# The order of the last group's stores, and of the last tile's second half on TensorE, in a fused attention and MLP kernel

## The chip, the cores and the metric

The kernel runs on one core of one Trainium2 chip. The metric is device time in microseconds (us) of one execution. The median of the three timed runs of the kernel before is 219.3 us (219.28 to 220.8). The profile is of one execution on its own, and has its own time.

## The reference

Two stages are computed one after the other. The first is a linear attention with a decay: for 4 batches and 8 heads of 768 positions and 64 columns, block by block, with a state that is carried from block to block. The second is an MLP on the 3072 rows that come out of it, with 512 columns in and out and 2048 in between:

```python
for b in range(nb):                     # 12 blocks of 64 positions
    intra = np.einsum('bhic,bhjc->bhij', qb, kb) * Dmask[None]
    intra = np.einsum('bhij,bhjd->bhid', intra, vb)
    inter = np.einsum('bhid,bhde->bhie', qb * lam_pow[None], kv_state)
    out[:, :, sl] = intra + inter
    kv_state = lam_block * kv_state + np.einsum('bhsd,bhse->bhde', kb_dec, vb)

h = x @ w_in                            # (3072, 512) @ (512, 2048)
s = np.sin(alpha * h)
g = h + s * s / (alpha + 1e-09)
return (g @ w_out).astype(np.float32)   # (3072, 2048) @ (2048, 512)
```

Only the last product and its way to memory are touched by the change.

## The kernel before, in words

The 3072 rows are worked in six groups of 512, numbered 0 to 5. For each group the attention part leaves its result transposed in a tile `xt`. The first MLP product (`f1`) makes 16 blocks of 128 of the 2048 middle columns, each with four matmuls (L689). ScalarE takes the sine (L696), ScalarE or GpSimd the square (L703, L705), and VectorE combines both into the tile `gall` (L708). The second product (`f2`) makes the output of the group in four row tiles, m = 0 to 3, each of 128 rows and 512 columns.

One row tile of `f2` is 16 matmuls that add up in one PSUM bank, in four blocks of four (`f2_g_m_j`, L725). A block takes as its weights four 128x128 pieces of `gall`, and multiplies them with 512 columns of `w_out_sb`. When the fourth block is done, ScalarE copies the bank to a buffer `ob` in SBUF (`ev_g_m`, L731). SyncE (SP) then issues two stores of 64 rows each, 128 KB each (`out_g_m`, L753).

The last row tile, group 5 and m = 3, is made differently (`make_f2_end`). It is cut into two halves of 256 columns, a and b, and each half has a bank of its own and four blocks of four matmuls (`f2_5_3_0a` to `f2_5_3_3a`, and the same with b). Half a is copied by ScalarE (`end0`, L737), and SP issues its two stores of 64 KB (`send0`, L746). Half b is copied by VectorE (`end1`, L739). Of its two stores (`send1`, L746) SP issues the first and ScalarE's queue the second:

```python
add("send0", on("SP", 1.0), [ev], lambda op, ev=ev, cols=cols:
    f2send(op, ev, g, m, cols, (SY, SY)))
...
add("send1", on("SP", 1.0), [ev], lambda op, ev=ev, cols=cols:
    f2send(op, ev, g, m, cols, (SY, A)))
```

What runs in what order is written out by hand. `SEQ` (L173 to L277) holds one list of names for each engine, SP among them. `Plan.run` walks the five lists with estimated costs, gives each operation its buffers, and emits the instructions in the order of the starts that it works out. Each engine therefore runs its own list in order. A waiting instruction holds everything behind it on the same engine. The waits themselves follow from the data: a copy waits for the matmuls of its bank, a store for its copy, and a copy for the stores that last read its `ob` buffer. There are three `ob` buffers (`NOB = 3`, L286), and the plan never gets back the one that `end0` takes.

The end of the five lists before the change is this:

- TensorE (L204, L205): three blocks of tile 1, the b half's first two blocks between the first and the second block of tile 0, and the b half's last two blocks at the very end. Tile 2 and the a half stand ahead of these.
- ScalarE (L253, L254): the copies `ev_5_2 end0 ev_5_1 ev_5_0`.
- VectorE (L223): `end1`.
- SP (L276): the stores `out_5_2 out_5_1 send1 send0 out_5_0`.

Of the kernel before, what the change touches and what calls it, by code (L numbers as in the profile page):

```python
# [145 lines left out]
def kernel(  # L146
# [59 lines left out]
        "DVE":  # L206
# [70 lines left out]
    }  # L277
    QS = set()
    CK0 = [("ACT", .62), ("DVE", .43)]
# [792 lines left out]
```

## Time and profile before

| what | value |
|---|---|
| timed runs, median of three | 219.3 us (219.28 to 220.8) |
| the profiled execution's own time | 218.37 us |
| its span, from the first to the last instruction | 216.6 us |
| TensorE (PE) busy | 206.4 us, 95% of the span |
| ScalarE (ACT) busy | 139.1 us, 64% |
| GpSimd (POOL) busy | 131.4 us, 61% |
| VectorE (DVE) busy | 119.4 us, 55% |
| stores of 128 KB that SP issues (L753) | 46, median 2.4 us from issue to landing |
| stores of 64 KB that SP issues (L746) | 3, median 2.0 us |
| stores of 64 KB that ScalarE's queue issues (L746) | 1, 2.2 us |

The span is what the trace covers, and 1.77 us of the execution's own time lie around it. Times of single instructions are given in us from the start of the span. The engines' busy times leave out the issuing of DMAs, the waits and the barrier at the end. So a stretch in which all engines are idle can still be work: stores that are issued, in flight, or waited for. "PEq", "SPq" and the like are the sequencers of the engines, which issue and wait.

### The profile page before, as it was taken

Reading aid. Unit: us, or ns where it says so; the run is one execution under the profiler, and the core shown is the slowest. Engines: PE = TensorE matmul, PEld = TensorE weight load, DVE = VectorE, ACT = ScalarE, POOL = GpSimd, SP = SyncE. Lnnn points to the kernel's source line nnn. Section 1 sums busy time; section 2 is a strip of 40 time slices with the busy share of each in tenths; the row PEclk is TensorE's granted clock in tenths of the full one; section 3 lists DMA queues with packets and bytes.
Section 4 is the critical chain, followed back from the end, with each engine's and each line's share of the span. In section 5 each row is a group of like instructions: output and inputs, shape, how many; then the busy total and the mean of one; then the engine's idle time right before and its main releaser. Section 6 shows DMA issues by size and latency. Waiting matters only on the chain.

```text
span 216.6 us, 5232 instructions
## 1 busy us (share of the span) xinstructions
PE 206.4 (95%) x2066; PEld 105.6 (49%) x2066; DVE 119.4 (55%) x174; ACT 139.1 (64%) x251; POOL 131.4 (61%) x212
## 2 busy tenths in 40 slices
PE   8889999999999999999999999999999999999970
PEld 3466444555445555455545555544444444445430
DVE  3487775385488754777958868773555223022000
ACT  3675788554998668979887787567587635442210
POOL 7999899488799789998979998231511120011000
PEclk9999999999999999999999999999999999999996
DMA  6999999999998999999888740042040120044424
GB/s 176 300 278 207 206 157 200 304 251 305 246 278 221 182 273 250 249 190 293 224 201 203 128 100 3 0 100 48 0 97 2 25 61 14 0 97 92 99 55 98
DMA packets 62139, 33.65 MB, mean 155 GB/s; under 512 B 17938, under 2 KB 59170, under 8 KB 62114
## 3 DMA queue, kind: packets, MB, share of 16 engines
q1 hardware_dynamic: 57776, 29.04, 57.9%
q0 software_dynamic: 4224, 4.19, 12.3%
q8 instruction: 16, 0.26, 0.5%
q10 hardware_dynamic: 114, 0.07, 0.1%
q14 instruction: 9, 0.07, 0.1%
HBM read 27.27 MB, written 6.29 MB: 155 GB/s over the span
## 4 chain that ended last, share of the span: by engine, by line
PE 87%; POOL 5%; DVE 2%; issue 2%; ACT 1%; POOLq 0%; DVEq 0%
PE hps L689 38%; PE ops L725 35%; PE okv L725 3%; PE sp L532 3%; PE okv L655 3%; PE okv L642 2%; POOL vb L498 1%; DVE gall L708 1%; PE okv L566 1%; PE pt L508 1%; POOL E L410 1%; ACT s L696 1%; ACT s L703 1%; DVE sm L540 1%; POOL w_in_sb L456 0%
## 5 line engine op out<-in xcount | busy, mean ns | idle before, releaser
L708 DVE SCALAR_TENSOR_TENSOR gall<-s,r_sb,hps 128x512 bf16<-128x512 bf16 (+1 forms) x97 | 69.6, 740 | 60.1 <-ACT s L703 42.9
L689 PE MATMUL hps<-xt,w_in_sb 128*128 128x512 bf16 (+1 forms) x388 | 91.7, 377 | 0.7 <-DVE gall L708 0.6
L696 ACT ACTIVATE s<-hps,alpha_sb 128x512 bf16<-128x512 f32 (+1 forms) x97 | 65.5, 680 | 29.0 <-PE hps L689 27.5
L725 PE MATMUL ops<-w_out_sb,gall 128*128 128x512 bf16 (+1 forms) x368 | 83.1, 370 | 0.0
L705 POOL TENSOR_TENSOR s<-s 128x512 bf16<-128x512 bf16 x31 | 32.1, 1041 | 49.3 <-ACT s L696 47.2
L725 PEld LDWEIGHTS <-gall 128*128 128x128 bf16 x400 | 38.5, 98 | 42.1 <-DVE gall L708 0.2
L689 PEld LDWEIGHTS <-w_in_sb 128*128 128x128 bf16 x388 | 36.4, 98 | 42.1 <-issue 1.8
L703 ACT ACTIVATE s<-s 128x512 bf16<-128x512 bf16 (+1 forms) x66 | 40.3, 621 | 1.2
L540 DVE TENSOR_TENSOR sm<-sp,mask 128x1024 bf16<-128x1024 f32 x24 | 29.2, 1218 | 1.0 <-PE sp L532 1.0
L498 POOL TENSOR_TENSOR vb<-st_v,R 128x512 bf16<-128x512 f32 x24 | 25.0, 1045 | 1.1 <-DMA st_v<-in_v_dram 0.9
L731 ACT COPY ob<-ops 128x512 f32<-128x512 f32 x21 | 12.2, 586 | 19.7 <-PE ops L725 19.7
L594 POOL TENSOR_TENSOR kvbd<-kvx,LBD 128x256 bf16<-128x256 f32 x32 | 19.7, 614 | 2.5
L674 DVE TENSOR_TENSOR xt<-okv,ET 128x512 bf16<-128x512 f32 x24 | 16.5, 687 | 6.1 <-ACT kva L576 3.6
L591 POOL TENSOR_TENSOR kvx<-kva,kvs 128x128 f32<-128x128 f32 x32 | 14.6, 456 | 7.3 <-ACT kva L576 7.2
L492 POOL CAST qk<-st_k 128x512 bf16<-128x512 f32 x18 | 10.9, 614 | 3.3 <-DMA st_k<-in_k_dram 3.2
L532 PE MATMUL sp<-qt 64*64 64x128 bf16 x384 | 10.1, 221 | 0.1
L655 PE MATMUL okv<-sm,vb 64*64 64x128 bf16 x384 | 9.7, 218 | 0.5 <-DVE sm L540 0.5
L490 ACT CAST qk<-st_q 128x512 bf16<-128x512 f32 x13 | 7.9, 619 | 3.1 <-DMA st_q<-in_q_dram 3.1
L576 ACT COPY kva<-okv 128x256 f32<-128x256 f32 (+1 forms) x16 | 5.1, 316 | 6.9 <-PE okv L566 6.9
L632 POOL TENSOR_TENSOR kvs<-kvx,ET 128x128 f32<-128x128 f32 x24 | 9.4, 404 | 0.0
L762 PE MATMUL bz<-const-bfloat16-1.0 128*128 128x256 bf16 (+1 forms) x33 | 8.3, 358 | 0.8 <-PEq L1056 0.8
L642 PEld LDWEIGHTS <-kvbd 128*128 128x128 bf16 x80 | 6.2, 98 | 5.3 <-POOL kvbd L594 0.5
(63 smaller groups left out, 109.5 us busy)
## 6 DMA issues: line engine op xcount, KB each, us to landing
st_k<-in_k_dram SPq DMA_DIRECT2D x24, 256.0 KB, 4.0
st_q<-in_q_dram SPq DMA_DIRECT2D x24, 256.0 KB, 5.1
st_v<-in_v_dram SPq DMA_DIRECT2D x24, 256.0 KB, 4.4
out_dram<-ob SPq DMA_DIRECT2D x46, 128.0 KB, 2.4
w_out_sb<-in_moe_w_out_dram POOLq DMA_DIRECT2D x4, 512.0 KB, 8.5
w_in_sb<-in_moe_w_in_dram POOLq DMA_DIRECT2D x2, 512.0 KB, 7.2
w_in_sb<-in_moe_w_in_dram POOLq DMA_DIRECT2D x1, 768.0 KB, 10.2
w_in_sb<-in_moe_w_in_dram POOLq DMA_DIRECT2D x1, 256.0 KB, 7.1
```

The source lines that it names most:

```text
L498: ENGINE[op.eng].tensor_tensor(out=T[u, "vb"][:], in0=T[u, "v"][:].rearrange("p h two e -> p two h e"), in1=R[:, :, hs].unsqueeze(3).to_br ...
L532: nc.tensor.matmul(out=T[u, "sp"][half[c], hd, par, hp, :], lhsT=QT[half[hd], 1, par, hp, half[c]], rhs=QT[half[hd], 0, :, hp, half[c]], s ...
L540: V.tensor_tensor(out=T[u, "sm"][:].rearrange("p hd par hp i -> p (hd par) hp i"), in0=T[u, "sp"][:].rearrange("p hd par hp i -> p (hd par ...
L594: G.tensor_tensor(out=bd[:], in0=X.unsqueeze(2).to_broadcast([P, 2, 2, D]), in1=LBD[:, hs, :].unsqueeze(3).to_broadcast([P, 2, 2, D]), op= ...
L655: nc.tensor.matmul(out=okv[half[hd], c, hp * P:(hp + 1) * P], lhsT=VB[half[c], par, 2 * hp + hd, :], rhs=ST[half[c], hd, par, hp, :], star ...
L674: V.tensor_tensor(out=o, in0=i, in1=ET[:, 2 * hh:2 * hh + 2].rearrange("p hp two e -> p hp (two e)") .unsqueeze(1).to_broadcast([P, 2, 2, ...
L689: op.ins = nc.tensor.matmul(out=op.tile[:, cols], lhsT=w_in_sb[:, c, f * P:(f + 1) * P], rhs=xt[g][:, c].rearrange("p b c i -> p (b c i)") ...
L696: A.activation(out=op.tile[:, cols], in_=mm.tile[:, cols], func=ACTF.Sin, scale=alpha_sb[:, f:f + 1])
L703: A.activation(out=op.tile[:, cols], in_=s1, func=ACTF.Square)
L705: ENGINE[op.eng].tensor_tensor(out=op.tile[:, cols], in0=s1, in1=s1, op=ALU.mult)
L708: V.scalar_tensor_tensor(out=gall[g][:, f, cols], in0=sq.tile[:, cols], scalar=r_sb[:, f:f + 1], in1=mm.tile[:, cols], op0=ALU.mult, op1=A ...
L725: op.ins = nc.tensor.matmul(out=first.tile[:, cols], lhsT=gall[g][:, f, m * P:(m + 1) * P], rhs=w_out_sb[:, f, cols], start=(f == 0), stop ...
```

## The change

In `SEQ`, two lists are written in another order. No instruction is added or taken away in the source, and no size changes.

- TensorE: the last three blocks of tile 0 move ahead of the b half's first two blocks, so that the b half is one block of 16 matmuls behind all full tiles.
- SP: `send0` moves ahead of `out_5_1`, and `send1` moves behind `out_5_0`. The list ends `out_5_2 send0 out_5_1 out_5_0 send1`.

In the built program ScalarE's and VectorE's instructions keep their order; SP's list and TensorE's differ as the diff says.

```diff
@@ -202,7 +202,7 @@
             "f2_5_3_0a f2_5_3_1a f2_5_2_1 f2_5_3_2a f2_5_3_3a f2_5_1_1 f2_5_2_2 f2_5_2_3 f2_5_1_2 "
-            "f2_5_0_0 f2_5_1_3 f2_5_3_0b f2_5_3_1b f2_5_0_1 f2_5_0_2 f2_5_0_3 f2_5_3_2b f2_5_3_3b ",
+            "f2_5_0_0 f2_5_1_3 f2_5_0_1 f2_5_0_2 f2_5_0_3 f2_5_3_0b f2_5_3_1b f2_5_3_2b f2_5_3_3b ",
@@ -273,7 +273,7 @@
-            "out_3_3 out_2_0 out_2_3 out_4_3 out_5_2 out_5_1 send1 send0 out_5_0 ",
+            "out_3_3 out_2_0 out_2_3 out_4_3 out_5_2 send0 out_5_1 out_5_0 send1 ",
```

## The prediction

> **What bounds the kernel now.** I read the page from the top: shares of engines, slices, chain. Then the last stretch of the trace alone, since the change touches nothing ahead of 205 us.
>
> ```profile
> PE 206.4 (95%) x2066; PEld 105.6 (49%) x2066; DVE 119.4 (55%) x174; ACT 139.1 (64%) x251; POOL 131.4 (61%) x212
> PE   8889999999999999999999999999999999999970
> SPq L1067 <- DMA out_dram<-ob: 1.6, 2, 1.0
> ```
>
> TensorE is the bound of the whole, at 95%. The second line is its busy share in 40 slices of 5.4 us: nothing moves it but the last slice, and that one reads 0. There it is not the bound any more. The third line is from the waits of SP's queue: SP stands at the kernel's end for its stores to land.
>
> The chain of waits from 195 us on and the timeline behind 209 us show what comes after TensorE:
>
> ```profile
> 195.88 13.87 PE ops L725 x80
> 209.75 0.03 DVEq L739
> 209.78 0.04 issue
> 209.83 0.42 DVE ob L739
> 210.28 1.75 SPq L746 DMA_DIRECT2D out_dram<-ob  x3
> 210.28 0.55 ACTq L746 DMA_DIRECT2D out_dram<-ob  x1
> 212.47 1.11 SPq L753 DMA_DIRECT2D out_dram<-ob  x2
> ```
>
> Columns are start, time, engine and line. TensorE ends at 209.75, the copy of half b at 210.25. The page's chain stops there, because issuing a DMA is not counted as work; the span goes on to 216.6. These 6.3 us are SP's: three stores of 64 KB in a row from 210.28 (one is `send1`, two are `send0`), then two of 128 KB (`out_5_0`) at 212.47 and 212.99. Two of these facts matter. `send0` was copied long ago, and `out_5_0` too:
>
> ```profile
> 203.37 0.38 ACT L737 COPY ob<-ops 128x256 f32<-128x256 f32 x1
> 205.44 0.59 ACT L731 COPY ob<-ops 128x512 f32<-128x512 f32 x1 [1.69 <-PE ops L725]
> 208.94 0.59 ACT L731 COPY ob<-ops 128x512 f32<-128x512 f32 x1 [2.92 <-PE ops L725]
> ```
>
> These are ScalarE's copies of half a, tile 1 and tile 0. They end at 203.75, 206.02 and 209.53, yet four stores of theirs are issued behind `send1`, because SP runs its list in order. The 212.99 store lands at 215.37 by the trace's landing records, and 1.22 later the span ends: SP checks the eight counters of its stores one by one (0.06 each), then comes the barrier.
>
> **The change part by part.** *SP's order.* No store is added: from `out_5_2` on SP issues nine before and nine after, and ScalarE's queue one. Their prices are in the rows: SP is taken 0.47 us by the first of a pair and 0.60 by the next, with 0.04 between; a pair is 1.11 (the 212.47 row).
>
> - `send0` in front of `out_5_1`: SP is free at 204.61, when `out_5_2` (203.50, two issues) is out. Two issues and a wait that is already met take it to about 205.8. `out_5_1` cannot go before its copy ends at 206.02, and goes at 206.05 as before. Cost: nothing, with 0.25 to spare; without that cover, up to 1.1 later for `out_5_1`, which lands at 208.91 now and is waited for by VectorE's copy (it gets the same `ob` buffer). That copy starts at 209.83, so 0.9 more is covered.
> - `out_5_0` in front of `send1`: its pair goes out as soon as its copy ends, below.
> - `send1` is last on SP, and the other half of it on ScalarE's queue is where it was, behind `ev_5_0`.
>
> *TensorE's order.* Matmuls start 0.109 us apart for 256 columns and 0.216 for 512 (starts of neighbouring weight loads). The eight matmuls of `f2_5_3_0b` and `1b` that stand between the blocks of tile 0 take 8 x 0.109 = 0.87, from 205.24 to 206.11. They go behind tile 0, so its copy starts at 208.94 - 0.87 = 208.07 and ends at 208.66. The sum of TensorE's work is the same, and its end stays 209.75: the moved blocks need `gall` blocks which the half a has already used, and a bank that the program frees with `end0`'s copy (203.75). Cost: nothing; should the bank be late, every us is a us at the end, but it has 4 us. ScalarE's copy of tile 0 also waits for `out_5_2` to have landed (same buffer), at 206.27: 1.7 of cover.
>
> *The sum.* `out_5_0` is issued at 208.69 and 209.20, SP is free at 209.79. Rows with the same pair (`out_5_1`, 206.05 and 206.57) land 2.24 and 2.35 behind their issues: 210.93 and 211.55. `end1` ends at 210.25 as now. SP and ScalarE's queue issue `send1` at 210.28, exactly as now, and these two landed at 212.25 and 212.50 in the trace of before. The last landing thus moves from 215.37 to 212.50. Behind it SP checks six counters more where it was five, as ScalarE's store falls on the second of them: 1.22 + 0.06 = 1.28. The span ends at 213.78 instead of 216.59: **2.8 us less**. With the 1.77 around the span, the profiled execution would have 215.56 instead of 218.37. The median of the runs shown, 219.3, stands 0.9 above that execution; I take 2.8 from it: **216.5 us** (-1.3%).
>
> Most of this is SP's order. With it alone, the `out_5_0` pair would go at 209.55 to 210.66 and the SP half of `send1` at about 210.70, some 0.4 later. TensorE's order alone is worth nothing: `out_5_0` would still go last.
>
> *Not in the trace: `send1` just behind a 256 KB pair in the same queue.* Before, it has nothing in flight ahead of it. The pair's packets ran from 1.12 behind its first issue to 2.51 behind it, here 209.80 to 211.20; `send1`'s packets began at 211.40. From below: ScalarE's half lands as early as SP's half did, 0.25 gained (less traffic follows it now: `send0` is gone). From above: `send1` begins only when the pair has landed at 211.55 and then needs its own 2.0 to 2.2: 213.77, which costs 1.27. The nearest row is the half store issued at 210.79 behind one at 210.28, which needed 2.06 against 1.97: 0.1. I take nothing, since 0.2 us lie between the packets.
>
> SP's rows show one gap without a wait: 212.03 to 212.47, where 0.04 is usual. Should it come again at the same place of the list, it falls in or behind the `out_5_0` pair, where SP has 0.49 us free (209.79 to 210.28). Price: nothing, or 0.2 if it meets `send1` (SP's half at 212.69 against 212.50).
>
> **The rivals.** *The last half waits behind the big pair* (the upper end above): 1.5 us gained, 217.8. For it: both use the same 16 DMA engines, whose share is 0.71 while a pair runs (205.24 to 206.11). Against it: the gap of 0.2, and the row with 0.1. The Trainium skill (DMA: Bandwidth & Descriptors, section "Queues, rings and completion order") speaks against the change here: the write that counts a store as done lands only after every earlier write of that DMA engine, across its queues. By that rule `send1` cannot be counted before `out_5_0` has been written; the trace of before does not show this pair of stores, and the landing estimate of 211.55 would leave the sum as it is.
>
> *The moved `send0` holds up `out_5_1`, and with it VectorE's copy* (the other side). One mechanism: two more stores in front in the same queue. `out_5_1` would have to land after 209.8 to cost anything, and after 212.6 (2.8 later) to make the kernel slower. Were the stores to run one behind the other, at the 3.6 us that the slowest store from 190 us on needed, `send0` would land at 208.3 and 211.9, `out_5_1` 2.35 later at 214.2. VectorE's copy would slip 4.4, the end 4.4 - 2.8 = 1.6: 220.9. Against it: the trace shows pairs landing 0.5 apart, as far as their issues are; in the window 206.11 to 208.69 the DMA share is 0.46.
>
> *It does not do what it says: the end does not move.* The last landing would have to be held by something that the rows do not show, such as longer waits between issues: 219.3. For it only the unexplained 0.44; the other stretches of SP's queue at the end are all named.
>
> **How the numbers follow.** The forecast, 216.5: 0.75. Last half behind the pair, 217.8: 0.13. No gain, 219.3: 0.08. Slower by `send0`, 220.9: 0.04. About 1% (2.2 us) is what a measurement of this kernel can tell from no change: the runs of before lie up to 0.7% apart. The forecast is only 0.6 us beyond that, so 0.05 of its chance goes to "within 1%". Faster by over 1%: 0.70. Within: 0.05 + 0.13 + 0.08 = 0.26. Slower: 0.04. The range goes from 215.6 (2.8 + 0.25 gained, and a median that stands 0.6 nearer to the profiled execution's own time) to 218.0 (just over the 217.8 rival). The cases above it have 0.12.
>
> **What the profile after would show.** Right: the 128 KB pair of tile 0 at about 208.7 and 209.2, ScalarE's copy ahead of it at 208.07; VectorE's copy still at 209.83; one store each on SP and ScalarE's queue at 210.28, and nothing behind; a span near 213.8. Wrong in the first rival's way: the two stores of 64 KB at 210.28 with more than 2.2 us to landing. In the second's: VectorE's copy later than 209.9, waiting for a DMA. TensorE's end off 209.75 would mean that the blocks are not free to move. A change anywhere ahead of 203 us would be none of this change's doing.

## The result

The changed kernel takes 216.01 us in the median of four runs (215.52 to 217.04), the kernel before 219.29 us (four runs, 218.63 to 220.8). The ratio is 0.987, with a 95% interval of 0.983 to 0.991. So it is faster, by 1.3% (0.9 to 1.7%). The profiled execution took 216.30 us, with a span of 214.5.

The profile after, first the busy time of the engines and TensorE's slices on the page, then the waits of SP's queue behind 195 us:

```profile
PE 205.4 (96%) x2037; PEld 106.5 (50%) x2066; DVE 119.4 (56%) x174; ACT 138.8 (65%) x251; POOL 131.2 (61%) x212
PE   8988999999999999999999999999999999999992
SPq L1067 <- DMA out_dram<-ob: 1.6, 2, 0.9
SPq L746 <- DVE ob L739: 0.4, 1, 0.4
```

Before, TensorE's last slice read 0, and now it reads 2: the stretch behind TensorE is shorter. In the last line SP waits for VectorE's copy for 0.4 us. The same line of the kernel before reads:

```profile
SPq L746 <- DVE ob L739: 3.0, 1, 3.0
```

While SP waited there, the stores of half a, copied long before, stood behind it. Now no store stands behind that wait. The chain of waits and the timeline show the order of the end (start, time, engine, line):

```profile
200.98 9.48 PE ops L725 x51
...
205.41 1.18 SPq L746 DMA_DIRECT2D out_dram<-ob  x2
206.76 3.74 SPq L753 DMA_DIRECT2D out_dram<-ob  x4
208.78 0.59 ACT L731 COPY ob<-ops 128x512 f32<-128x512 f32 x1 [2.05 <-PE ops L725]
210.54 0.42 DVE L739 COPY ob<-ops 128x256 f32<-128x256 f32 x1 [11.27 <-PE ops L725]
210.99 0.47 SPq L746 DMA_DIRECT2D out_dram<-ob  x1
210.99 0.55 ACTq L746 DMA_DIRECT2D out_dram<-ob  x1
```

The stores of half a now go at 205.41, ahead of tile 1's, and tile 0's two go at 209.39 and 209.91, the last two of the four at L753. TensorE ends at 210.46. Tile 0's copy starts 1.68 ahead of that (before: 0.8 ahead), half b's copy 0.08 behind it as before, and the last two stores go out together at 210.99, with nothing behind them. From here on **T** is TensorE's end in a run, and the **tail** is the time from T to the end of the span. The tail was 216.59 - 209.75 = 6.84 us and is 214.49 - 210.46 = 4.03 us: **2.81 us less**.

T itself is 0.71 later in the profile after. That is not the change, since the lag stands long before the changed code. Twenty weight loads in, TensorE is at 5.65 us in the trace of before and at 6.69 in that of after. The lag is 0.60 after 270 loads (18.81 and 19.41), 0.71 after 1600 (132.78 and 133.49), and 0.71 at the end. In both kernels the start is the same code. These two lines are the first 6 us, of before and then of after; the columns are engine busy times with instruction counts, PE and PEld first:

```profile
0.00:6.00 6.00, 5.23 (x23) 2.46 (x23) 2.13 (x12) 2.14 (x4) 4.38 (x17) 1.00 0.68 191
```

```profile
0.00:6.00 6.00, 5.23 (x15) 2.27 (x16) 2.13 (x12) 2.10 (x3) 4.37 (x17) 1.00 0.60 172
```

TensorE is busy for the same 5.23 us but has started 23 weight loads in one execution and 16 in the other. Over all eleven profiles in which TensorE is not stopped later, T lies between 209.7 and 210.7. The first 6 us alone do not set it: of the kernels below, the one with SP's order alone is 0.29 behind the kernel before after 20 loads, 0.93 after 270 and 0.99 at T, and the last one is 0.44 behind after 20 loads and level after 50. So T scatters by 1 us between executions whose code up to there is nearly the same, and that is why the tail says more here than the time. What makes the start quick or slow stays open.

### The profile page after: what moved, and what is told of

Read it like the earlier page. It is cut to its first block, busy times and chain, and to the rows that moved or that the text cites. A ratio compares the mean times of both kernels' runs of the same rounds, so it can differ in the third digit from the quotient of the medians.

```text
span 214.5 us, 5205 instructions
## 1 busy us (share of the span) xinstructions
PE 205.4 (96%) x2037; PEld 106.5 (50%) x2066; DVE 119.4 (56%) x174; ACT 138.8 (65%) x251; POOL 131.2 (61%) x212
## 4 chain that ended last, share of the span: by engine, by line
PE 91%; DVE 2%; ACT 2%; POOL 2%; issue 1%; DVEq 0%
PE hps L689 37%; PE ops L725 35%; PE sp L532 3%; PE okv L725 3%; PE okv L655 3%; PE bz L762 3%; PE okv L642 2%; PE pt L508 1%; DVE gall L708 1%; PE okv L566 1%; POOL vb L498 1%; ACT s L696 1%; ACT s L703 1%; DVE sm L540 1%; PE kp L566 0%
## 5 line engine op out<-in xcount | busy, mean ns | idle before, releaser
L689 PE MATMUL hps<-xt,w_in_sb 128*128 128x512 bf16 (+1 forms) x367 | 90.2, 377 | 1.8 <-DVE gall L708 0.5
L725 PE MATMUL ops<-w_out_sb,gall 128*128 128x512 bf16 (+1 forms) x362 | 82.1, 370 | 0.6 <-issue 0.5
L762 PE MATMUL bz<-const-bfloat16-1.0 128*128 128x256 bf16 (+1 forms) x33 | 9.4, 401 | 0.8 <-PEq L1056 0.8
L515 ACT COPY qt<-pt 128x512 bf16<-128x512 bf16 x11 | 6.4, 591 | 5.1 <-PE pt L508 5.1
```

The source lines that it names most:

```text
L689: op.ins = nc.tensor.matmul(out=op.tile[:, cols], lhsT=w_in_sb[:, c, f * P:(f + 1) * P], rhs=xt[g][:, c].rearrange("p b c i -> p (b c i)") ...
L725: op.ins = nc.tensor.matmul(out=first.tile[:, cols], lhsT=gall[g][:, f, m * P:(m + 1) * P], rhs=w_out_sb[:, f, cols], start=(f == 0), stop ...
```

## The experiments

All of them change the end of the lists or the stores alone. The time of the kernel before on the chips of these runs was 218.5 to 218.9 us.

### SP's order alone

```diff
 (from the kernel before)
-"... out_4_3 out_5_2 out_5_1 send1 send0 out_5_0 ",
+"... out_4_3 out_5_2 send0 out_5_1 out_5_0 send1 ",
```

> SP's new order alone, TensorE's order as before. Measured as the tail, from TensorE's end (T) to the end of the span: 6.84 us in the kernel before, 4.03 in the changed one. Theory (stores go out in SP's order, a store of 64 KB lands 2.0 to 2.2 after its issue, only packets in flight delay it): the pair of tile 0 goes at T - 0.2 to T + 0.9, SP's half of the last store at T + 0.95, it lands at about T + 3.1, tail 4.3; in time 2.5 less than the kernel before. Rival (the last half waits until the pair of 128 KB stores has landed): tail 5.9, in time about 1 less. Rival (TensorE's order carries the gain): tail 6.8, no gain.

Measured: 216.57 us against 218.82, ratio 0.989 (0.986 to 0.991). T is 210.74, the span 215.28, the tail 4.54. The timeline of the end:

```profile
209.93 0.59 ACT L731 COPY ob<-ops 128x512 f32<-128x512 f32 x1 [2.92 <-PE ops L725]
210.55 1.11 SPq L753 DMA_DIRECT2D out_dram<-ob  x2
211.28 0.55 ACTq L746 DMA_DIRECT2D out_dram<-ob  x1
211.77 0.53 SPq L746 DMA_DIRECT2D out_dram<-ob  x1
```

SP's half goes at T + 1.03 behind the pair, about as expected. It lands at T + 3.34 by the landing records, 2.31 behind its issue where it needs 1.96 undisturbed; ScalarE's half needs 2.59 in place of 2.21. So with the pair in flight ahead of it the last half comes 0.35 to 0.4 later. But the pair has landed at T + 2.70, and SP's half 0.64 later, not 2.0 later: the last half does not wait for the pair to land. Of the 2.8, SP's order alone brings 2.30.

### TensorE's order alone

```diff
 (from the kernel before)
-"f2_5_0_0 f2_5_1_3 f2_5_3_0b f2_5_3_1b f2_5_0_1 f2_5_0_2 f2_5_0_3 f2_5_3_2b f2_5_3_3b ",
+"f2_5_0_0 f2_5_1_3 f2_5_0_1 f2_5_0_2 f2_5_0_3 f2_5_3_0b f2_5_3_1b f2_5_3_2b f2_5_3_3b ",
```

> TensorE's new order alone, SP's order as before. Theory: the copy of tile 0 ends 0.9 earlier, but its pair of stores is still the last on SP behind the last half and the two stores of half a: tail 6.8 (down to 6.4 if the gap of 0.44 between issues does not come again), no gain in time. Rival (TensorE's order carries the gain): tail about 4, 2.8 less.

Measured: 218.64 us against 218.82, ratio 1.000 (0.997 to 1.002); T 209.90, tail 6.85. The timeline:

```profile
208.22 0.58 ACT L731 COPY ob<-ops 128x512 f32<-128x512 f32 x1 [2.05 <-PE ops L725]
210.43 1.76 SPq L746 DMA_DIRECT2D out_dram<-ob  x3
212.63 1.11 SPq L753 DMA_DIRECT2D out_dram<-ob  x2
```

Tile 0's copy is done at 208.80, and its stores go at 212.63: 3.8 us on the shelf. TensorE's order is worth nothing by itself, and 0.51 (4.54 - 4.03) on top of SP's, because it takes the pair out of the last half's way. Between the third and the fourth issue lies the gap of 0.44 again, at the same place of the list as before.

### The stores of half a behind tile 1's

```diff
 (from the changed kernel)
-"... out_5_2 send0 out_5_1 out_5_0 send1 ",
+"... out_5_2 out_5_1 send0 out_5_0 send1 ",
```

> The changed kernel with SP's two stores of half a behind tile 1's pair, where it was in front. Theory (moving them in front costs nothing, since SP is idle there and tile 1's pair lands 0.7 ahead of VectorE's copy): tail 4.0, the same time as the changed kernel. Rival (they hold up tile 1's pair, and through the shared buffer VectorE's copy): the copy starts earlier against T and the tail is shorter than 4.0.

Measured: 216.46 us, ratio 0.987 (0.985 to 0.990), tail 4.03. The place of `send0`, in front of `out_5_1` or behind it, neither costs nor brings anything; in both it is off the end of the list.

### Only the stores of half a moved

```diff
 (from the changed kernel)
-"... out_5_2 send0 out_5_1 out_5_0 send1 ",
+"... out_5_2 send0 out_5_1 send1 out_5_0 ",
```

> The changed kernel with only the stores of half a moved to the front of SP's end; the last half is issued ahead of tile 0's pair. Theory: the pair goes at T + 1.05 and T + 1.55 behind the last half, lands at T + 3.9, tail 5.1: of the 2.8 gained, the stores of half a make 1.7 and the place of the last half 1.1; in time 1.7 less than before. Rival (the last half behind the pair costs as much as it brings): tail 4.0 or less.

Measured: 217.48 us against 218.82, ratio 0.993 (0.991 to 0.995); T 210.12, span 215.39, tail 5.27. The timeline:

```profile
210.64 0.47 SPq L746 DMA_DIRECT2D out_dram<-ob  x1
210.65 0.55 ACTq L746 DMA_DIRECT2D out_dram<-ob  x1
211.22 1.17 SPq L753 DMA_DIRECT2D out_dram<-ob  x2
```

So 6.84 - 5.27 = 1.57 us come from taking the two stores of half a off the end (the gap of 0.44 that stood behind them no longer shows), and 5.27 - 4.03 = 1.24 from putting the last half behind tile 0's pair.

### The pair brought close to the last half

```diff
 (from the changed kernel)
-"f2_5_0_0 f2_5_1_3 f2_5_0_1 f2_5_0_2 f2_5_0_3 f2_5_3_0b f2_5_3_1b f2_5_3_2b f2_5_3_3b ",
+"f2_5_0_0 f2_5_1_3 f2_5_3_0b f2_5_3_1b f2_5_3_2b f2_5_0_1 f2_5_0_2 f2_5_0_3 f2_5_3_3b ",
```

> The changed kernel with three of the four blocks of half b ahead of tile 0's last three blocks on TensorE, so that tile 0's copy ends only at T + 0.2 and its pair of 128 KB stores meets the last half in the queues. Theory (only packets in flight delay a store): the pair's packets run from T + 1.4 to T + 2.8, SP's half follows and lands at about T + 3.6, tail about 4.9; the half on ScalarE's queue, issued at T + 0.5, shares the 16 DMA engines with the pair and lands later than 2.2 behind its issue. Rival (the last half waits until the pair has landed and then needs its own 2.0): tail 6.3.

Measured, in one run: 216.74 us, T 210.24, tail 4.71. The timeline:

```profile
210.32 0.42 DVE L739 COPY ob<-ops 128x256 f32<-128x256 f32 x1 [11.27 <-PE ops L725]
210.48 1.11 SPq L753 DMA_DIRECT2D out_dram<-ob  x2
210.77 0.54 ACTq L746 DMA_DIRECT2D out_dram<-ob  x1
211.71 0.52 SPq L746 DMA_DIRECT2D out_dram<-ob  x1
```

The pair's second store lands at T + 3.18, SP's half at T + 3.50, only 0.32 behind it and 2.02 behind its own issue. ScalarE's half, issued between the two stores of the pair, lands at T + 2.84, ahead of the second store and behind the first (T + 2.58). The rival of the prediction, with its 2.0 between the pair's landing and the half's, does not hold. In this run and in the one with SP's order alone the last four stores land in the order of their issue, here at T + 2.58, 2.84, 3.18 and 3.50; that agrees with the rule of the Trainium skill (DMA: Bandwidth & Descriptors, section "Queues, rings and completion order") that the write which counts a store lands after all earlier writes of its DMA engine. In these two runs the last halves come 0.06 to 0.4 later than undisturbed, whether by this rule or by the shared engines.

### A buffer that lands late

```diff
 (from the changed kernel)
-"... out_5_2 send0 out_5_1 out_5_0 send1 ",
+"... out_5_2 send0 out_5_0 out_5_1 send1 ",
```

> The changed kernel with tile 1's pair of stores behind tile 0's on SP. The plan then gives half b's copy the buffer of tile 0, so that VectorE's copy waits until tile 0's pair has landed. Theory (the wait for a buffer's stores is real, and has only 0.7 us of cover in the changed kernel): the pair lands at about T + 1.8, the copy starts there instead of T + 0.08, tail 5.8. Rival (such a wait costs nothing here): SP's half goes at T + 1.25 behind the two pairs, tail 4.7.

Measured, in one run: 217.50 us, T 209.74, tail 5.98. The chain of waits:

```profile
208.68 0.47 SPq L753
...
209.18 2.37 DMA out_dram<-ob
...
211.58 0.05 DVEq L739
...
211.68 0.05 DVEq L739
...
211.77 0.42 DVE ob L739
```

The chain runs through a store: tile 0's second store is issued at 209.18, lands 2.37 later, and only then VectorE finishes its checks of counters (the two DVEq pieces) and copies, at T + 2.03. This is the mechanism of the prediction's rival on the slower side, at work with a larger dose. It costs 1.95 of tail here, and the one run, 217.50 us, still lies below the kernel before on that chip (218.80), as the rival's own break-even of 2.8 says.

### Fewer counters behind the last landing

A counter is here the semaphore that a store raises as it lands. At the end SP checks eight of them in a fixed order, 0.06 us each. Which one a store counts on follows from how many stores were issued before it. Two kernels shift this by the same three places (five more stores are three fewer, modulo eight):

```diff
 (from the changed kernel, in f2st; the first kernel)
+        if (g, m) in ((3, 3), (2, 0), (2, 3)):
+            SY.dma_start(out=rows, in_=ev.tile[:])
+            return
```

> The changed kernel with three earlier tiles (3_3, 2_0, 2_3) stored by one transfer of 256 KB each in place of two of 128 KB, so that the stores' counters go round differently: ScalarE's last half gets the seventh of the eight counters that SP checks at the end, SP's half the eighth, where it was the second and the third. Theory (0.06 us for each counter checked behind the last landing): one counter is left behind the last landing in place of six, tail 4.03 - 0.3 = 3.7. In time 0.3 less than the changed kernel, 3.1 less than before, too little to be told from the changed kernel by the time alone. Rival (the checks are hidden or cost nothing): tail 4.0.

Measured: 222.59 us against 218.80 of the kernel before, ratio 1.018 (1.015 to 1.020): slower. The waits of all engines behind 170 us:

```profile
DVE ob L739 <- DMA out_dram<-ob: 15.9, 1, 15.9
ACT ob L731 <- DMA out_dram<-ob: 11.6, 3, 7.4
ACT ob L737 <- DMA out_dram<-ob: 4.5, 1, 4.5
```

Copies wait for stores, since the stores of 256 KB hold their `ob` buffers for long. In the window from 193 to 198 us, where one of them is in flight alone, the row of busy times reads:

```profile
193.00:198.00 5.00, 4.62 (x22) 1.98 (x21) 1.49 (x2) 1.18 (x3) 1.04 (x1) 1.00 0.11 41
```

The last two numbers are the busy share of the 16 DMA engines and GB/s: 0.11, near two of 16. A pair of 128 KB stores moves with a share of 0.71. The destination of the single transfer has a first axis of two (`two p d`). The Trainium skill (DMA: Bandwidth & Descriptors, section "Why a DMA increments its semaphore by 16 and not by 1") says that a transfer is spread over the largest number of engines, up to 16, that divides the slowest axis on both sides; with a two there that makes two engines, and the share agrees. The landing records agree too: this store has two at its landing, 197.70 and 197.76, where a store of 64 rows has sixteen. The counters themselves did what was expected, but nothing came of it: from the last landing at 219.53 to the end 0.98 us.

The second kernel shifts the counters by cutting stores instead:

```diff
 (from the changed kernel, in f2st; the second kernel)
         for par in range(2):
-            SY.dma_start(out=rows[par], in_=ev.tile[par * D:(par + 1) * D, :])
+            cut = (g, m) in ((3, 0), (4, 2)) or (g, m, par) == (4, 0, 0)
+            for c in ((slice(0, 256), slice(256, 512)) if cut else (slice(0, DM),)):
+                SY.dma_start(out=rows[par][:, c], in_=ev.tile[par * D:(par + 1) * D, c])
```

> The changed kernel with five of the 128 KB stores of earlier tiles (both of 3_0 and 4_2, one of 4_0) cut into two of 64 KB with 256 columns each, so that the last two stores again get the seventh and the eighth of the counters that SP checks at the end, this time without a transfer whose first axis has only two entries. Theory (0.06 us for each counter checked behind the last landing; what made the run with single transfers slow was their landing, not the counters): from the last landing to the end of the span 0.98 in place of 1.28, tail 3.7, time 0.3 less than the changed kernel. Rival (shifting the counters is what cost the time): slower than before, as with the single transfers.

> The changed kernel once more, on the same chip as the run with the cut stores, to set the two side by side: tail 4.0, time 2.8 less than the kernel before, as from the traces so far.

Measured on one chip: 215.97 us with the cut stores and 216.00 without, against 218.90 of the kernel before; ratios 0.987 (0.985 to 0.989) both. The rival, slower than before, does not hold. The tail is 4.04 in the changed kernel and 3.86 with the cuts. From the last landing to the end there are 0.96 us, as expected, but VectorE's copy started at T + 0.24 (T is 210.35). The chain of waits of the kernel with the cut stores shows why:

```profile
205.86 0.36 issue
206.22 0.47 SPq L746
...
207.38 2.36 DMA out_dram<-ob
...
209.76 0.02 DVEq L739
...
209.98 0.41 issue
210.39 0.05 DVEq L739
...
210.59 0.42 DVE ob L739
```

A gap of 0.36 between the two stores of half a makes `out_5_1` late: its second store is issued at T - 2.97, where it was T - 3.18 in the changed kernel. Yet it lands at T - 0.62, only 0.07 later than there (T - 0.69). Most of the time lies behind the landing, 0.86 us from 209.73 to the copy. Ahead of its copy VectorE makes five checks, about 0.1 us apart, in a fixed order of the counters. By the semaphores in the traces, the counter of this store is the fourth to be checked in the changed kernel. Here the shift has made it the first. So the other four checks, with a gap of 0.41 without a wait among them, come behind the landing. The next run shows which of the two made the copy late.

### Cut stores, and half a behind tile 1

```diff
 (from the kernel with the cut stores)
-"... out_5_2 send0 out_5_1 out_5_0 send1 ",
+"... out_5_2 out_5_1 send0 out_5_0 send1 ",
```

> The kernel with the five cut stores, and SP's two stores of half a behind tile 1's pair. In the run with the cut stores a gap of 0.36 us between the two stores of half a made tile 1's pair late, so that VectorE's copy started at T + 0.24 in place of T + 0.08 and gave back 0.16 of the 0.3. Theory: with the stores of half a behind tile 1's pair the copy is back at T + 0.08, 0.96 us lie between the last landing and the end, tail 3.7; in time 3.0 to 3.1 less than the kernel before. Rival (the cut stores themselves make VectorE's copy late): copy at T + 0.24 again, tail 3.9.

Measured: VectorE's copy back at T + 0.08, T 209.74, span 213.50, tail 3.76, the shortest of all. The stores of tiles 2 and 1, and VectorE's copy, in the timeline:

```profile
203.49 3.85 SPq L755 DMA_DIRECT2D out_dram<-ob  x4
209.81 0.42 DVE L739 COPY ob<-ops 128x256 f32<-128x256 f32 x1 [11.27 <-PE ops L725]
```

The outcome is as expected, but the reason given for it does not hold. Tile 1's second store, the last of the four, again goes behind a gap of 0.37, at 206.87, and lands at 209.12, which is T - 0.62, as late as in the run before this one. Yet the copy is 0.16 earlier against T. What differs is the counter: with `send0` behind it, this store has the one that VectorE checks third. So the 0.16 came from the place of the counter among VectorE's checks, that is from the shift by the cut stores, and not from the lateness of the landing.

The time is 216.15 us (215.31 to 218.0) against 218.51, ratio 0.991 (0.988 to 0.995). By the tail it is 0.27 better than the changed kernel; by time the scatter of the runs hides that, and the median is no lower.

## Why the prediction was right

It said 216.5 us, with 215.6 to 218.0 as its range and 2.8 us gained; the median is 216.01, and on the chip where both were run again the gain is 218.90 - 216.00 = 2.9.

- **The sum.** Last landing 2.75 behind T (210.46 to 213.21), forecast 2.75 (209.75 to 212.50); from there to the end 1.28, forecast 1.28. Tail 4.03, forecast 213.78 - 209.75 = 4.03. The span is 0.71 longer than forecast because T came 0.71 later, 0.60 of it within the first 20 us. By the medians of that measurement the time fell by 3.3, 0.5 more than forecast, which the tail does not show: 2.8 was taken from 219.3, and on the other chips the kernel before has medians of 218.5 to 218.9. The gain in the tail came as forecast; the level that it was taken from was not known that well.
- **TensorE's order is free**: its last 9.48 us are one unbroken piece of 51 matmuls, tile 1's copy starts at T - 4.30 in both profiles, and the copy of tile 0 moved from T - 0.80 to T - 1.68, 0.87 as worked out. Its worth was put at "some 0.4" and is 0.51.
- **SP's order carries the gain**: shown by either order alone, 2.30 and 0.
- **The last half behind a big pair**: at nothing, with 0.25 below and 1.27 above. In the changed kernel the halves land 1.96 and 2.21 behind their issue, the same as before: nothing. With the pair in the way it is 0.06 to 0.4, so the upper bound was too high by far, and the nearest row (0.1) was nearer, though up to 0.3 too low.
- **`send0` in front of `out_5_1`**: "nothing, with 0.25 to spare". SP was free 0.13 ahead of tile 1's copy end (206.60 against 206.73), and `out_5_1` went at the same T - 3.70. The cover was thinner than said, since the first of the two issues took 0.54 instead of 0.47. It held.
- **The cover of VectorE's copy** was misread. The prediction counts 0.9 from the landing of `out_5_1` to the copy, so that only a landing after 209.8 would cost. But VectorE still has checks to make behind that landing, with a gap of 0.42 among them in the trace of before. By an estimate from the times of these checks (the last starts at 209.41, and one that need not wait takes 0.05) they would have ended at 209.45, only 0.33 ahead of where TensorE's end let them. In the changed kernel the landing is 0.77 ahead of the copy, and by the same estimate the checks would have ended 0.55 early. In the kernel with the cut stores they end 0.16 late. The cost of nothing came true, with less room than stated.
- **The 0.44 gap** was put at "nothing, or 0.2", at the same place of the list. It is a gap of 0.36 to 0.37 (the rest is a check that was already met), and its place goes by count: in all six profiles in which it shows, it stands ahead of SP's 208th instruction in the trace, whatever that is. That is the check for tile 0's pair in the kernel before, the second store of half a with the cut stores, the second store of tile 0 in the kernel with half a behind tile 1. In the changed kernel the 208th is the first store of tile 0, which waits 1.45 for its copy anyway, so that a gap there would not show. VectorE's gap of 0.41 to 0.42 likewise stands ahead of its 192nd instruction, in the six profiles that show it. The cause of both stays open.
- **Two small readings** are off and change nothing: a pair's stores land 0.6 apart, not 0.5 (208.29 and 208.91), and `out_5_2` landed at 206.40 by its landing records, not at 206.27.

## What to carry to other kernels

Where the busiest engine ends ahead of the span, read the queue that issues the last stores in order, and ask of each store in it when its data was ready: here an in-order queue kept finished work behind a wait of 3.0 us. Put the stores in the order in which their data is ready, the one that waits for the last computation last, and give it a free queue; then look which buffer its copy waits for, and what the engine still checks behind that landing. In this kernel reordering the computation brought nothing before that, and 0.5 us after it, by clearing the last store's way.

## What was not expected of the hardware

A store whose destination has a first axis of two ran at a share of 0.11 of the DMA engines (41 GB/s). Three transfers of 256 KB in place of pairs of 128 KB brought the changed kernel to 222.59 us, 1.8% above the kernel before. Behind the last landing, 0.3 of 1.28 us at the end of the span depends on which counter the last store happens to use, and the same counters decide how many of VectorE's checks come behind a landing that its copy waits for. SP and VectorE each show a gap without a wait, 0.36 to 0.37 and 0.41 to 0.42, each ahead of the same instruction by count. And T differs by up to 1.0 us between executions that run nearly the same code up to there, which is a third of the gain measured here.
